# A fused spectral filter and spatial-shift MLP on one core: scales of three groups made at once, w2's scaling and memsets behind the second group's gelu scale, its statistics between the halves of w1

## The chip, the core and the metric

The kernel runs on one core of a Trainium2 chip. The metric is device time in microseconds of one execution. The kernel before takes 410.85 us (median of 3 runs, 410.72 to 411.11).

## What is computed

The input x has S = 2048 tokens of D = 448 features. The output is the sum of x, a spectral branch and an MLP branch:

```python
x = A_x
xn = _layernorm(x, axis=-1)
return x + _A_ref(xn, A_w_r, A_w_i) + _B_ref(xn, B_w1, B_w2, B_w3, B_w4)

def _A_ref(x, w_r, w_i):            # rfft2, times a complex weight, irfft2
    X = rfft2(x, axes=(-2, -1)) * (w_r + 1j * w_i)
    return irfft2(X, (S, D), axes=(-2, -1))

def _B_ref(x, w1, w2, w3, w4):
    h = _gelu(_layernorm(x, axis=-1) @ w1)
    # the four quarters of h's features are shifted by +1, -1, +2, -2 tokens
    hs = jnp.concatenate([g0, g1, g2, g3], axis=-1) @ w2
    x1 = x + hs
    h2 = _gelu(_layernorm(x1, axis=-1) @ w3) @ w4
    return x1 + h2
```

Only the first part of the MLP branch, up to the product with w2, is touched by the change. The spectral branch and the product with w3 and w4 follow it and overlap its end.

## The kernel before

**Tiling.** Token t sits in partition t // 16, so the 2048 tokens are 16 blocks of 128 partitions by 448 features. Blocks are worked on in four groups of four: `GRP = [[14, 15, 0, 1], [2, 3, 4, 5], [6, 7, 8, 9], [10, 11, 12, 13]]`. In this document they are called group 0 to group 3, as in the code. (The short description of the change counts them as words: its "third" group is group 2, its "second" is group 1.) All operands of matmuls are split into a high and a low float16 half, and a product is made of three passes: high by high, low by high, high by low. That is why most steps come in pairs, a copy on ScalarE (ACT) that makes the high half and a subtraction on VectorE (DVE) or GpSimd (POOL) that makes the low half.

**Steps of one group g, with their lines.**
- `stats` (L306, L307): mean and variance of each block on VectorE. The optional argument `pins` names, for each block, an instruction behind which its statistic is queued.
- `norm1` (L314 to L338): a first guess of the reciprocal root by integer arithmetic (`va`, `vy`: L323 to L326), the shift `nma` (L328), then the apply (L333 on ScalarE, L336 on VectorE or GpSimd, block by block as the list `apply` says). The result stands in place of x.
- `refine` (L345 to L354, all on GpSimd): ten small operations that make the root exact; the last one writes `gsc`, the scale that the gelu of this group's w1 product needs.
- `scales` (L358 to L365, all on GpSimd): eight small operations that make `cs`, by which the residual x is scaled when w2's product is added (L487), and the scale and bias with which the spectral branch later normalises x.
- `transpose_split` (called through `T1`; L387, L391, L401): sixteen transposes on TensorE, then high half on ScalarE and low half on VectorE. Group 3 goes through `turn` instead (L868 to L871), with a transpose by DMA.
- `w1_in` (L427): the product with w1, eleven matmuls for one block. A call for a part of the feature tiles does a part of it. The four units of group 0 keep their partial sums in the four banks of `first`.
- `w1_unit` (L467 to L478): gelu on ScalarE, high half on ScalarE (L468), low half on VectorE in two pieces (L470), both written, shifted, into `x2mem`; then one DMA transpose per finished block gives `h`.
- `w2_tile` (L486, L487): eleven matmuls with w2, then the residual on VectorE.
- `ln2`: the second layer norm of finished blocks and its DMA transposes (L506 to L522).

**Weights.** `squares` (L253, ScalarE) and `powers` (L258 to L267) turn the sum of squares of a weight into a power of two by which it is scaled: VectorE reduces (L258, marked "r1" or "r2" in the table `after`), TensorE adds over partitions by a product with ones (L260, "p1", "p2"), VectorE makes the exponent (L262 to L267, "e1", "e2"). The sum for w2 uses a free corner of the bank `first[0]`. `split_w` then makes the halves; for w2 and half of w1 GpSimd scales (L276, "ps"), ScalarE copies (L277) and GpSimd subtracts (L278). Two DMAs (L933, L934) copy parts of w2's high halves to other partitions.

**Shift over the ends.** `wrap_on` (L449 to L452) moves parts of group 0's result with two DMAs and clears one row of `pairs[0]` (L451) and all of `pairs[2]` (L452) on GpSimd; the areas are read and written again only when group 3's blocks are done (`wrap_back`).

**Order.** Each engine executes its own queue in order. The order in the queues comes from a planner that takes ready work in the order of the program and its priorities. `behind(key)` restricts it: every instruction that the block issues on the engine of a marked instruction is queued after that instruction. It is no wait of its own on another engine. `after["a1"]` stands for the last ScalarE copy and the last VectorE subtraction of group 1's transposes, `after["n", g]` for the last apply of group g on VectorE, `after["na", g]` for that on ScalarE, and `after["b0"]` for the last operations of `ln2([0, 1])`. SP's queue issues all DMAs.

Of the kernel before, what the change touches and what calls it, by code (L numbers as in the profile page):

```python
# [36 lines left out]
PIN = [("a3",), ("a3",), ("a3",), ("a3",)]  # L37
# [88 lines left out]
def body(tc, nc, x, wf, w1, w2, w3, w4, c_g, c_n, c_small, out):  # L126
# [185 lines left out]
    xn_scale, xn_bias = {}, {}  # L312

    def norm1(g, apply, pins=None):  # L314

        bs = GRP[g]
        n, b0 = len(bs), bs[0]
        mv = pc.tile([128, 4, 2], F32, name=f"mva{b0}")
        stats([xb(b) for b in bs], f"a{b0}", mv, pins)
        a = pc.tile([128, 2 * n], F32, name=f"va{b0}")  # L320
        yi = pc.tile([128, 2 * n], I32, name=f"vy{b0}")
        y = yi.bitcast(F32)
        V.tensor_scalar(out=a[:, n:], in0=mv[:, :n, 1], scalar1=1.0 + EPS, scalar2=EPS * EPS, op0=ALU.mult, op1=ALU.add)  # L323
        V.tensor_scalar(out=a[:, 0:n], in0=mv[:, :n, 1], scalar1=EPS, scalar2=None, op0=ALU.add)
        V.tensor_single_scalar(yi, a.bitcast(I32), 1, op=ALU.logical_shift_right)
        V.tensor_scalar(out=yi, in0=yi, scalar1=-1, scalar2=0x5F3759DF, op0=ALU.mult, op1=ALU.add)  # L326
        nm = pc.tile([128, n], F32, name=f"nma{b0}")
        i = V.scalar_tensor_tensor(out=nm, in0=mv[:, :n, 0], scalar=-1.0, in1=y[:, n:], op0=ALU.mult, op1=ALU.mult)  # L328
        after["c", g] = (i.ins,)
        for k, b in enumerate(bs):  # L330
            y_, m_ = y[:, n + k:n + k + 1], nm[:, k:k + 1]
            if apply[k] is A:
                i = A.activation(out=xb(b), in_=xb(b), func=AF.Identity, scale=y_, bias=m_)  # L333
                after["na", g] = (i.ins,)
            else:
                i = apply[k].tensor_scalar(out=xb(b), in0=xb(b), scalar1=y_, scalar2=m_, op0=ALU.mult, op1=ALU.add)  # L336
                if apply[k] is V:
                    after["n", g] = (i.ins,)  # L338

        q, z = (pc.tile([128, 2 * n], F32, tag=f"v{t}", bufs=2, name=f"v{t}{b0}") for t in "qz")  # L340
        w, r = (pc.tile([128, 2 * n], F32, name=f"v{t}{b0}") for t in "wr")
        nm1 = pc.tile([128, n], F32, name=f"nm{b0}")

        def refine():
            P.tensor_tensor(out=q, in0=y, in1=y, op=ALU.mult)  # L345
            P.tensor_tensor(out=q, in0=q, in1=a, op=ALU.mult)
            P.tensor_scalar(out=w, in0=q, scalar1=-10.0 / 3.0, scalar2=None, op0=ALU.add)
            P.tensor_tensor(out=w, in0=w, in1=q, op=ALU.mult)
            P.tensor_scalar(out=w, in0=w, scalar1=5.0, scalar2=None, op0=ALU.add)
            P.tensor_tensor(out=z, in0=w, in1=w, op=ALU.mult)  # L350
            P.tensor_tensor(out=z, in0=z, in1=q, op=ALU.mult)
            P.tensor_scalar(out=z, in0=z, scalar1=-0.5 * 0.375 ** 3, scalar2=1.5 * 0.375, op0=ALU.mult, op1=ALU.add)
            P.tensor_tensor(out=r, in0=z, in1=w, op=ALU.mult)
            P.tensor_scalar(out=gsc[:, 4 * g:4 * g + 4], in0=r[:, n:], scalar1=r1, scalar2=None, op0=ALU.mult)  # L354

        def scales():
            c, r1st, u = cs[:, 4 * g:4 * g + 4], w[:, 0:n], w[:, n:]
            P.tensor_tensor(out=r1st, in0=r[:, 0:n], in1=y[:, 0:n], op=ALU.mult)  # L358
            P.tensor_tensor(out=u, in0=r[:, n:], in1=r[:, n:], op=ALU.mult)
            P.tensor_tensor(out=c, in0=y[:, n:], in1=a[:, n:], op=ALU.mult)  # L360
            P.tensor_tensor(out=c, in0=c, in1=u, op=ALU.mult)
            P.tensor_tensor(out=c, in0=c, in1=r1st, op=ALU.mult)
            P.tensor_scalar(out=c, in0=c, scalar1=s12[:, 0:1], scalar2=None, op0=ALU.mult)
            P.tensor_tensor(out=nm1, in0=mv[:, :n, 0], in1=r1st, op=ALU.mult)
            P.tensor_scalar(out=nm1, in0=nm1, scalar1=-1.0, scalar2=None, op0=ALU.mult)  # L365
            for k, b in enumerate(bs):
                xn_scale[b], xn_bias[b] = r1st[:, k:k + 1], nm1[:, k:k + 1]
        return refine, scales
# [11 lines left out]
    def transpose_split(srcs, dst, key, ts=range(4), at=0, tags=("tr",) * 4, late=None):  # L380
        c = slice(128 * at, 128 * at + 128 * len(srcs))
        for t in ts:
            pt = bank(tags[t], f"pt{key}{t}")
            w = 128 if t < 3 else 64
            with behind("T", key) if ("T", key) in after else contextlib.nullcontext():
                for i, s in enumerate(srcs):
                    m = T.transpose(pt[:w, 128 * i:128 * i + 128], s[:, 128 * t:128 * t + w], ident)  # L387
# [3 lines left out]
            i = A.activation(out=dst[:w, t, c], in_=pt, func=AF.Copy)  # L391
            todo.append((key, t, i, lo, pt, dst[:w, t, c]))
        if late is None:
            low()

    todo = []

    def low():
        while todo:
            key, t, i, lo, pt, hi = todo.pop(0)  # L400
            j = V.tensor_tensor(out=lo, in0=pt, in1=hi, op=ALU.subtract)  # L401
            after[key, t] = after[key] = i.ins, j.ins
# [18 lines left out]
    def w1_in(g, units, ts, passes=range(3)):  # L421
        for p in passes:
            for t in ts:
                for i, pm in units:
                    wi, xi = ((0, 0), (0, 4), (4, 0))[p]
                    if t < 3 or p != 1:
                        T.matmul(pm[:, :D], xTs[g][:, xi + t, 128 * i:128 * i + 128], w1p[:, wi + t],  # L427
                                 start=t == 0 and p == 0, stop=t == 3 and p == 2)
# [20 lines left out]
    def wrap_on():  # L449
        move(pairs[1], pairs[0], -1)  # L450
        P.memset(pairs[0][0:1], 0.0)  # L451
        P.memset(pairs[2], 0.0)  # L452
# [403 lines left out]
    def T1(g, ts=range(4), late=None):  # L856
        if g not in xTs:
            xTs[g] = p1.tile([128, 7, 512], F16, tag="xT", bufs=2, name=f"xT{g}")
        transpose_split([xb(b) for b in GRP[g]], xTs[g], f"a{g}", ts,
                        tags=("mm", "mm", "tr", "tr") if g == 2 else ("tr", "tr", "acc", "acc"), late=late)  # L860
# [23 lines left out]
    n1 = [norm1(0, [P, V, A, V])]  # L884
    T1(0, range(1), True)
# [3 lines left out]
    with behind("e1"):  # L889
        low()  # L890
    for t in range(4):
        if t >= 1:
            with behind("p1"):
                T1(0, [t])
# [6 lines left out]
    n = 1  # L901
    for unit in list(enumerate(first))[:n]:
        w1_in(0, [unit], [2, 3])
    with behind("ps"):
        n1[0][0]()
    n1.append(norm1(1, [P, V, A, V], [("n", 0), ("r1",), ("a0", 0), ("a0", 1)]))
# [13 lines left out]
    n1[1][0]()  # L920
# [20 lines left out]
    n1[2][0]()  # L941
    for n in n1:
        n[1]()
# [16 lines left out]
    n1[0][0]()  # L960
    n1[0][1]()
# [153 lines left out]
```

## Time and profile before

| | |
|---|---|
| median of 3 runs | 410.85 us |
| the profiled execution | 410.88 us |
| its span on the core | 409.1 us |
| granted TensorE clock | 0.999 |
| busy: TensorE, VectorE, ScalarE, GpSimd | 400.4, 336.9, 256.1, 103.2 us |
| the first real matmul of w1 | at 12.44 us |
| DMA moved | 52.07 MB |

In the profile's rows PE is TensorE's matmul and PEld its weight load, DVE is VectorE, ACT ScalarE, POOL GpSimd, SP the queue that issues DMAs. A row of the time-ordered view has the start and the length in us, engine, line, operation, what it writes and reads, the shape, and how many like it were merged; in brackets stands how long the engine was idle before it and what ended the idle time. A row that merges several instructions covers the time from the first start to the last end. A row of the table by stages gives the stretch, its length, then busy time and number of instructions for PE, PEld, DVE, ACT and POOL, the granted clock, the share of DMA time, and GB/s. Names of buffers: `mva` mean and variance, `va` and `vy` the guess of the root, `nma` the shift, `vq`, `vz`, `vw`, `vr` the refinement, `pta` a bank of transposes, `xT` the transposed x, `w1s` and `w2s` weights as loaded, `w1p` and `w2p` their halves, `xr` a scratch target of the squares.

### The profile page before, as it was taken

Reading aid. Unit: us, or ns where it says so; the run is one execution under the profiler, and the core shown is the slowest. Engines: PE = TensorE matmul, PEld = TensorE weight load, DVE = VectorE, ACT = ScalarE, POOL = GpSimd, SP = SyncE. Lnnn points to the kernel's source line nnn. Section 1 sums busy time; section 2 is a strip of 40 time slices with the busy share of each in tenths; the row PEclk is TensorE's granted clock in tenths of the full one; section 3 lists DMA queues with packets and bytes.
Section 4 is the critical chain, followed back from the end, with each engine's and each line's share of the span. In section 5 each row is a group of like instructions: output and inputs, shape, how many; then the busy total and the mean of one; then the engine's idle time right before and its main releaser. Section 6 shows DMA issues by size and latency. Waiting matters only on the chain.

```text
span 409.1 us, 8749 instructions
## 1 busy us (share of the span) xinstructions
PE 400.4 (98%) x3391; PEld 297.5 (73%) x3391; DVE 336.9 (82%) x702; ACT 256.1 (63%) x434; POOL 103.2 (25%) x173
## 2 busy tenths in 40 slices
PE   8899999999999999999999999999999999999996
PEld 3455545765667777877787887877777779998995
DVE  5998999999856895998798888956899999965645
ACT  4689699882558866655598878863454445453431
POOL 7787630112145948310022111110000000000000
PEclk9999999999999999999999999999999999999999
DMA  8977995558779652536255666510011023100101
GB/s 275 373 286 139 238 177 140 110 115 178 102 200 292 219 151 77 182 136 179 68 144 143 155 149 164 146 31 13 22 70 69 24 85 96 46 2 2 45 2 45
DMA packets 54596, 52.07 MB, mean 127 GB/s; under 512 B 35678, under 2 KB 48542, under 8 KB 54556
## 3 DMA queue, kind: packets, MB, share of 16 engines
q1 hardware_dynamic: 54556, 51.53, 46.4%
q8 instruction: 26, 0.43, 0.4%
q14 instruction: 14, 0.11, 0.1%
HBM read 38.28 MB, written 3.67 MB: 103 GB/s over the span
## 4 chain that ended last, share of the span: by engine, by line
PE 86%; DVE 5%; DMA 3%; POOL 2%; ACT 1%; SPq 1%; issue 1%
PE pw L407 33%; PE acc L816 23%; PE pw L486 6%; PE side L786 4%; PE acc L786 3%; PE pu L675 3%; PE ps L575 3%; PE pe L696 2%; PE pp L630 2%; PE px L647 2%; PE py L717 2%; PE pw L427 2%; DMA xt<-x 1%; DVE sta L306 1%; DVE xT L401 1%; DMA w2p<-w2p 1%
## 5 line engine op out<-in xcount | busy, mean ns | idle before, releaser
L407 PE MATMUL pw<-x2mem,w3p 128*128 128x256 f16 x1232 | 152.0, 273 | 0.0
L407 PEld LDWEIGHTS <-w3p 128*128 128x128 f16 x1232 | 119.0, 98 | 19.6
L816 PE MATMUL acc<-w4p,hf 128*128 128x448 f16 (+1 forms) x516 | 104.2, 348 | 0.0
L816 PEld LDWEIGHTS <-hf 128*128 128x128 f16 x516 | 50.1, 98 | 37.5
L734 ACT ACTIVATE pw<-pw,pe 128x512 f32<-128x512 f32 x42 | 27.5, 654 | 31.7 <-PE pw L407 31.6
L737 DVE SCALAR_TENSOR_TENSOR hf<-pw,h,hf 128x512 f16<-128x512 f32 x42 | 31.3, 745 | 12.7 <-ACT hf L736 12.4
L486 PE MATMUL pw<-w2p,h 128*128 128x448 f16 x176 | 35.7, 353 | 1.6 <-DMA h<-x2mem 1.2
L427 PE MATMUL pw<-w1p,xT 128*128 128x448 f16 x176 | 34.8, 352 | 0.7 <-ACT w1p L280 0.4
L656 POOL TENSOR_TENSOR z<-te 128x450 f32<-128x450 f32 x16 | 15.7, 981 | 70.7 <-DVE te L654 65.8
L736 ACT ACTIVATE hf<-pw,h 128x512 f16<-128x512 f32 x42 | 28.8, 685 | 5.0 <-PE acc L816 4.0
L486 PEld LDWEIGHTS <-h 128*128 128x128 f16 x176 | 17.1, 98 | 17.2 <-DMA h<-x2mem 1.9
L427 PEld LDWEIGHTS <-xT 128*128 128x128 f16 x176 | 17.2, 98 | 16.6 <-issue 1.1
L752 ACT ACTIVATE hz<-g,h 128x896 f16<-128x896 f32 x14 | 14.6, 1042 | 22.9 <-DVE g L749 22.9
L786 PEld LDWEIGHTS <-hz 128*128 128x128 f16 x294 | 28.2, 98 | 0.6
L637 ACT ACTIVATE pf<-pp 64x450 f16<-64x450 f32 x32 | 17.3, 542 | 12.6 <-DVE pf L638 9.6
L638 DVE TENSOR_TENSOR pf<-pp,pf 64x450 f16<-64x450 f32 x32 | 19.9, 622 | 5.1 <-ACT pf L637 4.8
L753 DVE SCALAR_TENSOR_TENSOR hz<-g,h,hz 128x896 f16<-128x896 f32 x14 | 16.1, 1147 | 6.7 <-ACT hz L752 6.7
L558 POOL TENSOR_TENSOR f<-xr 128x452 f32<-128x452 f32 x16 | 19.7, 1250 | 0.6
L566 DVE TENSOR_TENSOR xh<-f,xh 128x452 f16<-128x452 f32 x16 | 14.3, 916 | 4.9 <-ACT xh L565 4.9
L652 ACT ACTIVATE te<-px 64x450 f32<-64x450 f32 x32 | 17.3, 540 | 1.2 <-PE px L647 0.6
L746 ACT ACTIVATE g<-pw,pe 128x512 f32<-128x512 f32 x14 | 9.6, 683 | 11.4 <-PE pw L407 11.4
L555 POOL TENSOR_TENSOR xr<-xf 128x452 f32<-128x452 f32 x8 | 9.2, 1154 | 24.4 <-issue 17.6
(188 smaller groups left out, 712.5 us busy)
## 6 DMA issues: line engine op xcount, KB each, us to landing
wc<-wf SPq DMA_DIRECT2D x32, 225.0 KB, 3.7
wl<-wf SPq DMA_DIRECT2D x8, 450.0 KB, 4.2
xt<-x SPq DMA_DIRECT2D x8, 448.0 KB, 7.8
xf<-x SPq DMA_DIRECT2D x8, 448.0 KB, 4.9
loads<-x SPq DMA_DIRECT2D x7, 448.0 KB, 3.5
out<-xt SPq DMA_DIRECT2D x13, 224.0 KB, 1.9
w3raw<-w SPq DMA_DIRECT2D x3, 896.0 KB, 11.3
gn<-c_g SPq DMA_DIRECT2D x16, 128.0 KB, 3.1
```

The lines of the kernel that those rows point to most:

```text
L407: T.matmul(ps_out, wp[:, wi + t, cols], xT[:, xi + t, tok], start=t == 0 and wi + xi == 0, stop=t == 3 and wi == 4)
L427: T.matmul(pm[:, :D], xTs[g][:, xi + t, 128 * i:128 * i + 128], w1p[:, wi + t], start=t == 0 and p == 0, stop=t == 3 and p == 2)
L486: T.matmul(pm[:, :D], h[:, k], w2p[:, w], start=n == 0, stop=n == 10)
L558: P.tensor_tensor(out=f[:, :, k:k + 2].rearrange("p b s d -> p s b d"), in0=u[:, :, 0], in1=u[:, :, 1], op=op)
L637: A.activation(out=hi, in_=src, func=AF.Copy)
L638: V.tensor_tensor(out=lo, in0=src, in1=hi, op=ALU.subtract)
L652: A.activation(out=e[64 * h:64 * h + 64], in_=px_[64 - 64 * h:128 - 64 * h, :2 * DF], func=AF.Copy)
L734: A.activation(out=pm, in_=pm, func=AF.Gelu_apprx_tanh, scale=r3)
L736: i = A.activation(out=h[:, 0], in_=pm, func=AF.Copy, scale=h3)
L737: j = V.scalar_tensor_tensor(out=h[:, 1], in0=pm, scalar=h3, in1=h[:, 0], op0=ALU.mult, op1=ALU.subtract)
L786: m = T.matmul(to, h[:, hi, 128 * blk:128 * blk + 128], b[wi], start=new and n == 0, stop=n == 2 and (last if blk in (2, 5, 3, 0) else end ...
L816: m = T.matmul(to, h[:, hi, o:o + 128], w4p[0][:, wi, f, r], start=first and f % 2 == 0 and n == 0, stop=end and f % 2 == 1 and n == 2, sk ...
```

## The change

- `mva`, `va`, `vy`, `vw`, `vr` and the two shifts become one tile each for all groups; a group uses a slice.
- `scales(g, n)` works on n groups at once: one call for groups 0 to 2 after group 2's `refine`, instead of three calls there, and one for group 3.
- Group 0 is applied by `[P,V,P,V]` instead of `[P,V,A,V]`, and all its transposes stand behind "p1"; the first four had stood ahead of it, with their low half behind "e1".
- Group 1's statistics are pinned behind "r1", the first copy of group 0's transposes, and the first two halves of w1, instead of group 0's last apply, "r1" and the first two copies. Group 2's are pinned behind "e2" as well.
- Two units of group 0 (n = 2, before 1) finish their w1 product ahead of "p2"; the last two, before three, stand behind "p2" and not behind group 1's transposes. "p2" itself stands behind the matmuls of the second unit.
- w2's scaling on GpSimd is queued behind group 1's `gsc`, and the two memsets of `wrap_on` behind w2's last low half.
- w3's splits and the squares of w4 beside them stand behind "b0" and not behind "a3".

```diff
-PIN = [("a3",), ("a3",), ("a3",), ("a3",)]
+PIN = [("b0",), ("b0",), ("b0",), ("b0",)]
...
+    mva = pc.tile([128, NB, 2], F32, name="mva")
+    va, vw, vr = (pc.tile([128, 2, NB], F32, name=f"v{t}") for t in "awr")
+    vyi = pc.tile([128, 2, NB], I32, name="vy")
...
-            P.tensor_scalar(out=gsc[:, 4 * g:4 * g + 4], in0=r[:, n:], scalar1=r1, scalar2=None, op0=ALU.mult)
-
-        def scales():
-            c, r1st, u = cs[:, 4 * g:4 * g + 4], w[:, 0:n], w[:, n:]
...
+            i = P.tensor_scalar(out=gsc[:, c], in0=r[:, 1], scalar1=r1, scalar2=None, op0=ALU.mult)
+            after["g", g] = (i.ins,)
+        return refine
+
+    def scales(g, n):
+
+        o = slice(4 * g, 4 * g + 4 * n)
+        c, r1st, u, y, r = cs[:, o], vw[:, 0, o], vw[:, 1, o], vy[:, :, o], vr[:, :, o]
+        P.tensor_tensor(out=r1st, in0=r[:, 0], in1=y[:, 0], op=ALU.mult)
+        P.tensor_tensor(out=u, in0=r[:, 1], in1=r[:, 1], op=ALU.mult)
+        P.tensor_tensor(out=c, in0=y[:, 1], in1=va[:, 1, o], op=ALU.mult)
+        P.tensor_tensor(out=c, in0=c, in1=u, op=ALU.mult)
+        P.tensor_tensor(out=c, in0=c, in1=r1st, op=ALU.mult)
+        P.tensor_scalar(out=c, in0=c, scalar1=s12[:, 0:1], scalar2=None, op0=ALU.mult)
+        P.tensor_tensor(out=nm1[:, o], in0=mva[:, o, 0], in1=r1st, op=ALU.mult)
+        P.tensor_scalar(out=nm1[:, o], in0=nm1[:, o], scalar1=-1.0, scalar2=None, op0=ALU.mult)
...
     def wrap_on():
         move(pairs[1], pairs[0], -1)
-        P.memset(pairs[0][0:1], 0.0)
-        P.memset(pairs[2], 0.0)
...
-    n1 = [norm1(0, [P, V, A, V])]
-    T1(0, range(1), True)
+    n1 = [norm1(0, [P,V,P,V])]
     with behind("n", 0):
         s1, r1 = powers(m1, 4, "1", "mm")
     first = [bank("mm" if k < 2 else "sp", f"pw1_0{k}") for k in range(4)]
-    with behind("e1"):
-        low()
     for t in range(4):
-        if t >= 1:
-            with behind("p1"):
-                T1(0, [t])
+        with behind("p1"):
+            T1(0, [t])
...
-    n = 1
+    n = 2
...
-    n1.append(norm1(1, [P, V, A, V], [("n", 0), ("r1",), ("a0", 0), ("a0", 1)]))
+    n1.append(norm1(1, [P, V, A, V], [("r1",), ("a0", 0), ("w1", 0), ("w1", 1)]))
...
     with behind("T", "a1"):
-        for unit in list(enumerate(first))[n:]:
+        for unit in list(enumerate(first))[n:2]:
             w1_in(0, [unit], [2, 3])
-    with behind("n", 1):
+    with behind("n", 1), behind("u"):
         s2, r2 = powers(m2, 1, "2", first[0][:, 448:512])
+    with behind("p2"):
+        for unit in list(enumerate(first))[2:]:
+            w1_in(0, [unit], [2, 3])
...
     with behind("a1"):
-        n1.append(norm1(2, [P, V, A, P]))
+        n1.append(norm1(2, [P, V, A, P], [("e2",), ("e2",), ("e2",), ("e2",)]))
...
     wrap_on()
-    with behind("na", 2):
+    with behind("g", 1), behind("na", 2):
         for k in range(4):
             r = slice(0, 128 if k < 3 else 64)
-            split_w(w2p[r, k], w2p[r, 7 + k], w2s[r, k], s2[r], P)
+            after["w2", k] = split_w(w2p[r, k], w2p[r, 7 + k], w2s[r, k], s2[r], P)
         SY.dma_start(w2p[64:128, 3:7], w2p[0:64, 0:4])
         SY.dma_start(w2p[0:64, 4:7], w2p[64:128, 0:3])
+    with behind("w2", 3):
+        P.memset(pairs[0][0:1], 0.0)
+        P.memset(pairs[2], 0.0)
...
-    n1[2][0]()
-    for n in n1:
-        n[1]()
+    n1[2]()
+    scales(0, 3)
```

More of the change, by code (lines that the diff above doesn't have):

```diff
@@ L391, in transpose_split @@
             i = A.activation(out=dst[:w, t, c], in_=pt, func=AF.Copy)
[L392 to L401 removed]
+            j = V.tensor_tensor(out=lo, in0=pt, in1=dst[:w, t, c], op=ALU.subtract)
             after[key, t] = after[key] = i.ins, j.ins
@@ L426, in w1_in @@
                     if t < 3 or p != 1:
-                        T.matmul(pm[:, :D], xTs[g][:, xi + t, 128 * i:128 * i + 128], w1p[:, wi + t],
-                                 start=t == 0 and p == 0, stop=t == 3 and p == 2)
+                        m = T.matmul(pm[:, :D], xTs[g][:, xi + t, 128 * i:128 * i + 128], w1p[:, wi + t],
+                                     start=t == 0 and p == 0, stop=t == 3 and p == 2)
+        after["u"] = (m.ins,)
     def slot(b):
```

62 lines of the change are left out of this document (24 added, 38 removed).

## The prediction

> **What bounds the kernel now.** I read the page's busy times first, then the table by stages, then TensorE's waits, and last the time-ordered rows of each engine over the first 62 us, where every edited line runs.
>
> ```profile
> span 409.1 us, 8749 instructions
> PE 400.4 (98%) x3391; PEld 297.5 (73%) x3391; DVE 336.9 (82%) x702; ACT 256.1 (63%) x434; POOL 103.2 (25%) x173
> ```
> ```profile
> 9.16:24.80 15.64, 13.22 (x81) 8.29 (x81) 13.80 (x42) 11.61 (x23) 12.17 (x33) 1.00 1.03 379
> ...
> 37.69:58.35 20.66, 19.86 (x105) 10.03 (x104) 19.63 (x60) 17.19 (x28) 10.81 (x32) 1.00 1.00 208
> 58.35:120.00 61.65, 61.65 (x394) 38.50 (x395) 55.05 (x146) 44.90 (x71) 8.73 (x19) 1.00 0.68 143
> ```
>
> TensorE (second column) is full from 58.35 on: later time is a fixed amount of matmul. Only the idle before 58.35 can be won, unless the change starves TensorE later. That idle is short, and TensorE's rows in time order name each piece in brackets (how long, and what ended it):
>
> ```profile
> 10.32 0.38 PE L260 MATMUL pm<-pt,ones 128*128 128x1 f32 x2 [0.50 <-DVE pt L258]
> ...
> 12.44 1.67 PE L427 MATMUL pw<-w1p,xT 128*128 128x448 f16 x8 [0.37 <-ACT w1p L280]
> 14.46 4.13 PE L427 MATMUL pw<-w1p,xT 128*128 128x448 f16 x21 [0.34 <-DVE w1p L281]
> 19.34 0.38 PE L260 MATMUL pw<-pt,ones 128*128 128x1 f32 x2 [0.75 <-DVE pt L258]
> 20.18 1.97 PE L387 MATMUL pta<-ident,xt 128*128 128x128 f32 x16 [0.46 <-POOL xt L336]
> ...
> 35.12 1.31 PE L486 MATMUL pw<-w2p,h 128*128 128x448 f16 x6 [0.51 <-DMA h<-x2mem]
> ...
> 37.69 0.73 PE L486 MATMUL pw<-w2p,h 128*128 128x448 f16 x3 [0.45 <-DMA w2p<-w2p]
> ...
> 58.35 2.25 PE L486 MATMUL pw<-w2p,h 128*128 128x448 f16 x11 [0.68 <-DMA h<-x2mem]
> ```
>
> Together 4.06 us, the most that tidying can give. The 21 matmuls in 4.13 us give 0.197 us for one w1 matmul and 0.113 us (sixteen in 1.8 us, the last one's modelled end left out) for one transpose. Groups are numbered 0 to 3 in this text.
>
> **The change part by part.**
>
> *Group 0's fourth apply moves from ScalarE to GpSimd; the sum that scales w1 comes sooner.*
>
> ```profile
> 8.46 0.74 ACT L333 ACTIVATE xt<-xt,nma,vy 128x448 f32<-128x448 f32 x1
> 9.11 0.56 ACT L253 ACTIVATE xr<-w1s 64x448 f16<-64x448 f32 x1
> ```
> ```profile
> 8.09 1.26 DVE L336 TENSOR_SCALAR xt<-xt,vy,nma 128x448 f32<-128x448 f32 x2
> 8.16 0.94 POOL L336 TENSOR_SCALAR xt<-xt,vy,nma 128x448 f32<-128x448 f32 x1
> ...
> 10.12 0.14 DVE L258 TENSOR_REDUCE pt<-m 128x1 f32<-128x4 f32 x1
> ...
> 12.01 0.62 DVE L306 BATCH_NORM_STATS2 sta<-xt 128x6 f32<-128x448 f32 x1
> ...
> 13.19 0.62 DVE L306 BATCH_NORM_STATS2 sta<-xt 128x6 f32<-128x448 f32 x1
> 13.72 0.68 DVE L281 SCALAR_TENSOR_TENSOR w1p<-w1s,pe,w1p 128x448 f16<-128x448 f32 x1
> ...
> 20.87 0.60 ACT L391 ACTIVATE xT<-pta 128x512 f16<-128x512 f32 x1 [0.26 <-PE pta L387]
> ```
>
> Without L333 the fourth square starts 0.65 us earlier. The first statistic of group 1 is now pinned behind the reduction L258 and not ahead of it, so L258 starts when VectorE's applies end, 9.35 instead of 10.12: 0.77 us. Against it: GpSimd does two applies in a row, the second at the 0.71 us of group 1's (row below), and ends at 9.8, and all sixteen transposes now stand behind the small matmul. Four transposes later, near 10.4, ScalarE's first copy (L391, 0.60 us) can start; the copy of w1 is as long. The first w1 matmul comes at 11.6 if w1's copy goes second on ScalarE, at 12.2 if third, instead of 12.44: 0.2 to 0.8 us, I take **-0.5**. The 0.34 us wait for the low half L281 goes too (**-0.34**; bounds 0 and -0.34): two statistics stood ahead of it, and the new pins hold one of them back behind w1's halves.
>
> *n = 2: two units' tail matmuls ahead of the w2 sum, two behind it, none behind group 1's transposes.* Five more matmuls, 5 x 0.197 = 0.98 us, stand where TensorE waited 0.75 us, and ten (1.97 us) where it waited 0.46 us for GpSimd's apply of group 1. Both waits are covered: **-1.21**. But TensorE reaches the w2 sum at 18.59 - 0.84 + 0.98 = 18.7, and if VectorE's reduction stays where it is, it still waits until 19.34, 0.6 us. Two things pull it forward:
>
> ```profile
> 16.76 1.03 POOL L278 TENSOR_TENSOR w1p<-w1s,w1p 128x448 f16<-128x448 f32 x1
> ...
> 16.79 1.03 DVE L325 TENSOR_SCALAR vy<-va 128x8 int32<-128x8 int32 x1
> ...
> 18.32 0.20 POOL L358 TENSOR_TENSOR vw<-vr,vy 128x4 f32<-128x4 f32 x1
> ...
> 19.42 0.71 POOL L336 TENSOR_SCALAR xt<-xt,vy,nma 128x448 f32<-128x448 f32 x1
> ...
> 29.15 0.17 DVE L325 TENSOR_SCALAR vy<-va 128x8 int32<-128x8 int32 x1
> ```
>
> L325 takes 0.17 us at 29.15; at 16.79 it was held until GpSimd's L278 ended. And L336 stood behind scale operations of group 0 (from L358 at 18.32 on, up to 1.1 us) that now run after group 2. I take half: **+0.3** left of the wait (0 to 0.6).
>
> The price: before, fifteen tail matmuls covered the evacuation of group 1's transposes. Now ten do if the transposes go first, none if they go last. Uncovered, TensorE waits for four copies of 0.6 us and their low halves less the transposes' own time, about 1 us. Bounds 0 and +1.0; program order puts the transposes first, so **+0.3**.
>
> *Three groups' scales at once; w2's scaling behind group 1's gelu scale; memsets behind w2's split.*
>
> ```profile
> 5.55 1.60 POOL L452 MEMSET x2mem<- 128x1792 f16 x1
> ...
> 22.68 1.25 POOL L276 TENSOR_SCALAR w2s<-w2s,pe 128x448 f32<-128x448 f32 x2
> ...
> 25.46 0.20 POOL L353 TENSOR_TENSOR vr<-vz,vw 128x8 f32<-128x8 f32 x1
> ...
> 27.49 1.58 POOL L451 MEMSET x2mem<- 1x1792 f16 x1
> ...
> 28.09 1.01 DVE L323 TENSOR_SCALAR va<-mva 128x4 f32<-128x4 f32 x1
> ...
> 30.42 1.96 ACT L277 ACTIVATE w2p<-w2s 128x448 f16<-128x448 f32 x4
> ...
> 32.90 3.01 POOL L278 TENSOR_TENSOR w2p<-w2s,w2p 128x448 f16<-128x448 f32 x3
> ...
> 37.63 0.29 POOL L354 TENSOR_SCALAR gsc<-vr,pe 128x4 f32<-128x4 f32 x1
> ...
> 39.13 0.29 POOL L363 TENSOR_SCALAR cs<-cs,s 128x4 f32<-128x4 f32 x1
> ...
> 40.97 0.66 DVE L487 SCALAR_TENSOR_TENSOR xt<-xt,cs,pw 128x448 f32<-128x448 f32 x1
> ```
>
> Sixteen small GpSimd operations vanish (24 become 8; at 0.20 to 0.29 us, L358 and L363, 3 to 4.6 us). A 12-wide one is not in the trace; 8-wide L353 and 4-wide L358 both take 0.20, so I price it the same, and at 0.30 as the upper end. w2's scaling (four of 0.63 us) can wait: its reader L277 starts at 30.42, 6.5 us after it ended. With the memset gone from 27.5, L323 and L324 shed the 0.9 us by which they were held, so group 2's chain (statistics, apply, w2's high halves, w2p's DMA, the first transpose of h) moves at least as far as TensorE does. Hence I leave the waits of 0.51 and 0.45 as they are: **0** (bounds -0.96 and, if w2's halves stay, +1.0). The DMAs of w2p and the shift, and SP's order of them, are not pinned anew.
>
> The memsets add 1.58 + 1.60 us between w2's last low half (32.90 + 3.01 = 35.9) and the rest of group 2's refinement (to the end of L354, 2.0 us) and the scales (to the end of L363, 1.5 us). If the low halves end 1.45 us earlier, cs is ready at 34.45 + 3.2 + 2.0 + 1.6 = 41.25; L487 asks for it at 40.97 - 1.45 = 39.5. So L487 waits, and in VectorE's queue group 3's aggregates and normalisation, and with them SP's run of DMA transposes, may stand behind it:
>
> ```profile
> 43.38 0.15 DVE L323 TENSOR_SCALAR va<-mva 128x4 f32<-128x4 f32 x1
> ...
> 49.79 2.56 SPq L871 DMA_TRANSPOSE xT<-x  x2
> ...
> 55.17 1.25 SPq L478 DMA_TRANSPOSE h<-x2mem  x1
> ```
>
> That run is full from 49.79 to the h that TensorE waits for at 58.35. Loss 0 if group 3's work goes ahead of L487, up to 1.45 + 0.3 = 1.75 us if behind. I take **0**: group 3's statistics come first in the program.
>
> The GPSIMD Engine Reference of the Trainium skill (Specifications) says that GpSimd contends with VectorE only for instructions in a two-port mode or with two SBUF inputs. The held L323 and L325 agree. By it the memsets' new place is free beside PSUM evacuations, and costs up to 1.6 us only if it meets group 3's short scalar chain at 43.4.
>
> *The rest.* e2 in front of group 2's statistics changes nothing, since these already stand behind group 1's last low half. Moving w3's splits behind b0 instead of a3 changes no more: they need s3, made from all of w3's squares, the last of which is pinned behind a unit of group 2. What can move is the squares of w4 in the same blocks: one that gets ahead of group 3's copies on ScalarE costs that chain some 1.1 us (twice the columns of L253 above); one that fills a gap costs nothing. I take **0**, since the copies come first in the program.
>
> **Sum:** -0.5 - 0.34 - 1.21 + 0.3 + 0.3 = -1.45 us. The profiled execution took 410.88, 1.78 over its span; 410.88 - 1.45 = 409.43, and it lies 0.03 over the median. I say **409.4**.
>
> **The rivals.**
>
> *Given back at SP (410.8).* TensorE comes early and waits for the same h at 58.35: 0.68 becomes about 2.1 us. For it: VectorE is busy 19.63 of 20.66 us there, and the cs arithmetic above. Against: with cs late, group 3's chain has a free VectorE.
>
> *Slower: GpSimd's pile-up (412.2).* If the early chain does not move, cs comes at 35.9 + 3.2 + 2.0 + 1.6 = 42.7, 1.7 us after L487's start; with L487 ahead of group 3's aggregates all of SP's run slips by as much, less some 0.3 us won elsewhere: +1.4. It decides from where cs passes 41.0 while group 3 stands behind L487. For: the memsets come earlier in the program than refinement and scales. Against: the 0.9 us hold on L323 is gone in any case.
>
> *More (408.0).* The w2 sum moves a full microsecond (-0.3 more), the evacuation is covered (-0.3), and the three DMA waits shrink by half of 1.64 us: -2.9.
>
> *Pins without effect.* If the order on VectorE comes out as before, only the n = 2 part and ScalarE's freed time act: about -0.7, 410.2; it belongs to the same class as no change.
>
> **How the numbers follow.** Forecast 0.42, more 0.13, no change (both kinds) 0.20, slower 0.25. A difference under 0.2% (0.8 us) cannot be told from none. So faster 0.55, same 0.20, slower 0.25. The forecast's own range is 408.7 to 410.0; with the cases of both signs, 407.7 to 412.1.
>
> **What would show it.** Right: first w1 matmul near 12, the w2 sum near 18.9, no wait there above 0.4, group 1's unit matmuls done 1 to 2 us before 33.15, and the 58.35 row earlier by the same. Wrong: a wait of w1 matmuls for L401 or L391 near 22, cs (L363) after 42 with L487 just behind it, a hold on L323 near 43, or the row at 58.35 unmoved behind a longer wait for h.

## The result, and the profile after

| | before | changed |
|---|---|---|
| median, side by side | 410.98 us (410.72 to 411.59, 4 runs) | 408.26 us (408.05 to 408.32, 4 runs) |
| profiled execution | 410.88 | 408.05 |
| its span | 409.1 | 406.3 |

The changed kernel takes 0.9931 of the time before, with an interval of 0.9914 to 0.9948: faster by 2.7 us, where 1.45 was forecast.

TensorE's rows in time order, of the profile after (row form as before; L389 are the transposes, L420 the product with w1, L478 that with w2):

```profile
9.54 0.38 PE L260 MATMUL pm<-pt,ones 128*128 128x1 f32 x2 [0.37 <-DVE pt L258]
...
11.72 6.92 PE L420 MATMUL pw<-w1p,xT 128*128 128x448 f16 x34
19.30 1.97 PE L389 MATMUL pta<-ident,xt 128*128 128x128 f32 x16 [0.66 <-POOL xt L336]
21.10 0.28 PE L260 MATMUL pw<-pt,ones 128*128 128x1 f32 x2
21.24 10.37 PE L420 MATMUL pw<-w1p,xT 128*128 128x448 f16 x54
31.45 1.91 PE L389 MATMUL pta<-ident,xt 128*128 128x128 f32 x16
33.72 1.31 PE L478 MATMUL pw<-w2p,h 128*128 128x448 f16 x6 [0.36 <-DMA h<-x2mem]
...
37.39 2.26 PE L478 MATMUL pw<-w2p,h 128*128 128x448 f16 x11 [0.28 <-DMA h<-x2mem]
...
46.67 4.33 PE L478 MATMUL pw<-w2p,h 128*128 128x448 f16 x22
51.21 2.25 PE L478 MATMUL pw<-w2p,h 128*128 128x448 f16 x11 [0.22 <-DMA h<-x2mem]
...
53.44 2.24 PE L420 MATMUL pw<-w1p,xT 128*128 128x448 f16 x11
55.52 2.25 PE L478 MATMUL pw<-w2p,h 128*128 128x448 f16 x11
```

Two more rows of before, to lay beside these (33.15, the transposes of group 2, answers to 31.45, 55.43 to 53.44, 58.35 of the prediction to 55.52):

```profile
33.15 1.47 PE L387 MATMUL pta<-ident,xt 128*128 128x128 f32 x12
...
55.43 2.24 PE L427 MATMUL pw<-w1p,xT 128*128 128x448 f16 x11
```

So the lead over before is 0.72 us at the first w1 matmul, 1.70 at 31.45, 1.99 at 53.44 and 2.83 at 55.52. The span is shorter by 2.8: all of it was won before 58 us, and the lead keeps its size from there on. The brackets of these two executions say where:

- 0.72 at the first matmul, and 0.34 because no wait for L281 stands among the 34 matmuls.
- Behind them, waits of 0.75 and 0.46 became one of 0.66: 0.55. With 0.09 in gaps too short for a bracket this makes the 1.70.
- Waits for h and w2's parts, 0.51 + 0.45, became 0.36 + 0.28 + 0.22: 0.10, and 0.19 more in short gaps.
- The 0.68 for h at 58.35 is gone, with 0.16 around it: 0.84.

GpSimd's rows of the changed kernel, and some of VectorE's, hold the part of the change that the prediction feared (the first row of each belongs to group 1 and is used further below):

```profile
18.30 0.94 POOL L336 TENSOR_SCALAR xt<-xt,vy,nma 128x448 f32<-128x448 f32 x1
...
35.15 1.58 POOL L927 MEMSET x2mem<- 1x1792 f16 x1
36.68 1.58 POOL L928 MEMSET x2mem<- 128x1792 f16 x1
...
40.30 0.21 POOL L360 TENSOR_TENSOR vw<-vr,vy 128x12 f32<-128x12 f32 x1
...
41.81 3.19 POOL L336 TENSOR_SCALAR xt<-xt,vy,nma 128x448 f32<-128x448 f32 x4
...
45.16 0.31 POOL L365 TENSOR_SCALAR cs<-cs,s 128x12 f32<-128x12 f32 x1
```
```profile
16.92 0.58 DVE L324 TENSOR_SCALAR va<-mva 128x4 f32<-128x4 f32 x1
...
39.99 0.17 DVE L324 TENSOR_SCALAR va<-mva 128x4 f32<-128x4 f32 x1
...
45.51 1.27 DVE L479 SCALAR_TENSOR_TENSOR xt<-xt,cs,pw 128x448 f32<-128x448 f32 x2 [0.29 <-POOL cs L365]
```

The scales `cs` are ready at 45.47, 6 us later than before (39.42), and the residuals L479 start right behind them. But group 3's chain went ahead of the residuals: its L324 runs at 39.99, against 43.38 before (L323 there). TensorE feels nothing: the third tile of w2 needs the PSUM bank that the first residual frees, near 46.2 (estimated as half of the row), and its turn comes only at 46.67. SP's queue of the changed kernel shows what group 3's early chain does to the order there:

```profile
44.65 1.82 SPq L863 DMA_TRANSPOSE xT<-x  x1
46.57 1.83 SPq L470 DMA_TRANSPOSE h<-x2mem  x1
48.51 2.85 SPq L863 DMA_TRANSPOSE xT<-x  x2
51.45 1.25 SPq L470 DMA_TRANSPOSE h<-x2mem  x1
...
59.80 2.56 SPq L514 DMA_TRANSPOSE x2mem<-y  x2
```

Before, the h that TensorE waited for at 58.35 was issued at 55.17 behind two transposes of x and two of the second norm:

```profile
52.52 2.56 SPq L522 DMA_TRANSPOSE x2mem<-y  x2
```

Now it is issued at 51.45, with no transpose of the second norm ahead of it.

### The profile page after: what moved, and what is told of

It is laid out like the page before. It is cut to its first block, busy times and chain, and to the rows that moved or that the text cites. A ratio compares the mean times of both kernels' runs of the same rounds, so it can differ in the third digit from the quotient of the medians.

```text
span 406.3 us, 8732 instructions
## 1 busy us (share of the span) xinstructions
PE 399.9 (98%) x3391; PEld 297.2 (73%) x3391; DVE 333.6 (82%) x702; ACT 255.1 (63%) x433; POOL 100.4 (25%) x158
## 2 busy tenths in 40 slices
DMA packets 54596, 52.07 MB, mean 128 GB/s; under 512 B 35678, under 2 KB 48542, under 8 KB 54556
## 4 chain that ended last, share of the span: by engine, by line
PE 87%; POOL 5%; DMA 2%; DVE 2%; ACT 2%; issue 1%; SPq 0%; POOLq 0%; ACTq 0%
PE pw L400 33%; PE acc L808 23%; PE pw L478 6%; PE side L778 4%; PE acc L778 3%; PE pu L667 3%; PE ps L567 3%; PE pe L688 2%; PE pp L622 2%; PE px L639 2%; PE py L709 2%; PE pw L420 2%; DMA w1s<-w 1%; POOL xt L336 1%; DMA h<-x2mem 1%
## 5 line engine op out<-in xcount | busy, mean ns | idle before, releaser
L400 PEld LDWEIGHTS <-w3p 128*128 128x128 f16 x1232 | 118.9, 98 | 19.3
L729 DVE SCALAR_TENSOR_TENSOR hf<-pw,h,hf 128x512 f16<-128x512 f32 x42 | 31.3, 746 | 12.9 <-ACT hf L728 12.7
L478 PE MATMUL pw<-w2p,h 128*128 128x448 f16 x176 | 35.8, 353 | 0.9 <-DMA h<-x2mem 0.9
L420 PE MATMUL pw<-w1p,xT 128*128 128x448 f16 x176 | 34.9, 352 | 0.1
L478 PEld LDWEIGHTS <-h 128*128 128x128 f16 x176 | 17.0, 98 | 17.0 <-DMA h<-x2mem 2.0
L420 PEld LDWEIGHTS <-xT 128*128 128x128 f16 x176 | 17.1, 99 | 16.1 <-DVE xT L394 0.4
```

What stands on the lines that cost most here:

```text
L400: T.matmul(ps_out, wp[:, wi + t, cols], xT[:, xi + t, tok], start=t == 0 and wi + xi == 0, stop=t == 3 and wi == 4)
L420: m = T.matmul(pm[:, :D], xTs[g][:, xi + t, 128 * i:128 * i + 128], w1p[:, wi + t], start=t == 0 and p == 0, stop=t == 3 and p == 2)
L478: T.matmul(pm[:, :D], h[:, k], w2p[:, w], start=n == 0, stop=n == 10)
L729: j = V.scalar_tensor_tensor(out=h[:, 1], in0=pm, scalar=h3, in1=h[:, 0], op0=ALU.mult, op1=ALU.subtract)
```

## The experiments

Each is the changed kernel with the edit shown, except the last of the first part; each ratio is to the kernel before on the same chip, which took 410.9 to 411.0 us there.

### GpSimd's small operations

**Scales group by group, as early as the data allow.** The merging undone.

```diff
-    scales(0, 3)
+    for g in range(3):
+        scales(g, 1)
```

> The changed kernel (span 406.3 us, 2.8 less than before) with the scales of groups 0, 1 and 2 as three separate calls again at the same place of the program, so that the planner may put each where it is ready. Theory A (the late cs let group 3's normalisation go ahead of the first residual on VectorE, which filled SP's run earlier and took away the 0.68 us wait for h at 58 us): cs of group 0 is there before 30 us again, the first residual (L479) stands ahead of group 3's scalar chain, L324 of group 3 goes from 39.99 to 42 or later, and the wait for h near 55 to 58 us comes back; time 0.7 to 1.2 us over the changed kernel's 408.26 us, 409.0 to 409.5. Theory B (GpSimd's relief: six small operations of group 0 in front of group 1's apply): group 1's transposes start about 1.2 us later than 19.30 and the time is 1.0 to 1.3 us over, with group 3's chain in its early place. Theory C (only the earlier arrival of w1's sum and the two-unit order count): within 0.4 us of 408.26.

Measured 409.78 us (409.36 to 411.86), ratio 0.9982 [0.9969, 0.9994]: 1.5 us of the gain gone. GpSimd's and TensorE's rows of this run:

```profile
18.51 0.21 POOL L360 TENSOR_TENSOR vw<-vr,vy 128x4 f32<-128x4 f32 x1
...
20.44 0.71 POOL L336 TENSOR_SCALAR xt<-xt,vy,nma 128x448 f32<-128x448 f32 x1
```
```profile
21.21 1.97 PE L389 MATMUL pta<-ident,xt 128*128 128x128 f32 x16 [2.10 <-POOL xt L336]
```

Small operations of group 0 stand ahead of group 1's apply again, from 18.51 on. The apply starts at 20.44 instead of 18.30, and the wait of 0.66 becomes 2.10: 1.44 us more, about the size of the loss. The first residual went ahead of group 3's chain, as theory A had it (L479 at 41.50, L324 at 44.00), but no wait for h near 55 to 58 us came back, and the time lies above the ranges of both theories.

**The same 24 operations, but all behind group 2's refinement.** The place kept, only the merging undone.

```diff
-    scales(0, 3)
+    with behind("g", 2):
+        for g in range(3):
+            scales(g, 1)
```

> The changed kernel with three separate calls of scales as in scales_apart, but queued on GpSimd behind group 2's gelu scale, where the one call stands. The number of GpSimd operations is that of before, their place that of the change. Theory A: cs is as late as in the changed kernel or later, group 3's chain goes first, 408.0 to 408.7 us. Theory B asks only for the place ahead of group 1's apply to be free, which it is: the same. If it is the merging itself that counts (sixteen operations of 0.2 us in front of group 3's four applies), the applies start up to 4 us later than 41.81 and the time is 1 us or more over 408.26.

Measured 412.52 us (411.3 to 413.49), ratio 1.0037 [1.0023, 1.0051]: slower than before. The first scale `cs` comes at 48.44 here, and the third tile of w2 has run into it:

```profile
48.47 1.27 DVE L479 SCALAR_TENSOR_TENSOR xt<-xt,cs,pw 128x448 f32<-128x448 f32 x2 [0.36 <-POOL cs L365]
```
```profile
49.20 6.00 PE L478 MATMUL pw<-w2p,h 128*128 128x448 f16 x22 [2.38 <-DVE xt L479]
```

A wait of 2.38 us, and then 22 matmuls take 6.00 us that take 4.33 in the changed kernel (row at 46.67). So the late place alone loses; the changed kernel bears it because merging takes sixteen operations, and 3 us, out of the stretch ahead of `cs`.

**Two groups' scales early, behind group 1's gelu scale.**

```diff
+    with behind("g", 1):
+        scales(0, 2)
     for k in range(4):
         w1_unit(1, k)
...
-    scales(0, 3)
+    scales(2, 1)
```

> The changed kernel with the scales of groups 0 and 1 made together behind group 1's gelu scale, those of group 2 alone in the old place. cs of the first residuals is there 15 us earlier than in the changed kernel, but no scale operation stands ahead of group 1's apply. memsets_back (cs at 39.2, residual ahead of group 3's chain, 408.56) has spoken against theory A; if the 1.5 us of scales_apart came only from the six operations ahead of group 1's apply (theory B), this one stays within 0.4 us of 408.26 with transposes of group 1 at 19.3; if an early cs costs, it is at 409 or above.

Measured 408.84 us (408.51 to 408.95), ratio 0.9945 [0.9933, 0.9958]. Nothing of the scales stands ahead of group 1's apply, TensorE's wait there is 0.73 us, and all but 0.6 us of the gain stays (theory B allowed 0.4; the interval overlaps that of the changed kernel). Late scales are not needed for most of it; scales out of the way at 18 to 20 us are.

**The kernel before with this one part.** Its scales, group by group, queued behind group 1's apply; nothing else of the change.

```diff
-                if apply[k] is V:
-                    after["n", g] = (i.ins,)
+                after["n" if apply[k] is V else "np", g] = (i.ins,)
...
     for n in n1:
-        n[1]()
+        with behind("np", 1):
+            n[1]()
```

> The kernel before with one part alone: the scales of groups 0 to 2, still one group at a time, are queued on GpSimd behind group 1's apply. Theory B (the small operations ahead of that apply cost the time there): the apply runs near 18.6 instead of 19.42, the waits of 0.75 and 0.46 us at 18.6 to 20.2 fall below 0.4 together; if nothing else moves 410.0 to 410.4. Rival: the planner now queues the w2 sum behind group 1's transposes on TensorE, so s2 and w2's scaling come later and TensorE waits for w2's parts between 33 and 40: 410.8 to 412.5.

Measured 411.05 us (410.77 to 411.35), ratio 1.0004 [0.9995, 1.0013]: nothing won. The apply did move up, from 19.42 to 18.63, and the planner then put the w2 sum behind the transposes on TensorE:

```profile
19.81 1.97 PE L386 MATMUL pta<-ident,xt 128*128 128x128 f32 x16 [1.11 <-POOL xt L336]
21.61 3.00 PE L426 MATMUL pw<-w1p,xT 128*128 128x448 f16 x15
24.45 0.28 PE L260 MATMUL pw<-pt,ones 128*128 128x1 f32 x2
```

The two waits there fell from 1.21 to 1.11 us only, since five matmuls fewer than in the changed kernel (29, not 34) stand ahead of the transposes and the apply lasts 1.13 us here. And the sum is 5 us later, w2's parts with it; the three waits for h and w2's parts grew from 1.64 to 2.28 us. Alone the part wins nothing; it pays only beside the other edits.

### The memsets, the late scales and the pins

**The memsets back in `wrap_on`.**

```diff
         move(pairs[1], pairs[0], -1)
+        P.memset(pairs[0][0:1], 0.0)
+        P.memset(pairs[2], 0.0)
...
-    with behind("w2", 3):
-        P.memset(pairs[0][0:1], 0.0)
-        P.memset(pairs[2], 0.0)
```

> The changed kernel with the two memsets of the wrap in their old place in the program (behind nothing). GpSimd then has 3.2 us less between w2's last low half and the scales, so cs would be there up to 3 us before 45.5. Theory A: if cs is early enough for the planner to put the first residual ahead of group 3's chain, part of the gain goes, 408.6 to 409.3 us; if not, within 0.3 us of 408.26. My GpSimd pile-up theory of the prediction (memsets in that place cost time) says faster than the changed kernel by 0.3 to 1 us.

Measured 408.56 us (408.36 to 408.6), ratio 0.9942 [0.993, 0.9954], an interval that overlaps the changed kernel's. `cs` is ready at 39.18, the residuals go ahead of group 3 as before, and SP's run of transposes begins at 48.07:

```profile
48.07 2.56 SPq L865 DMA_TRANSPOSE xT<-x  x2
50.80 1.22 SPq L516 DMA_TRANSPOSE x2mem<-y  x1
52.07 1.29 SPq L472 DMA_TRANSPOSE h<-x2mem  x1
```

There is still no wait for h near 55: its issue at 52.07 stands behind one transpose of the second norm, not two. So neither the late scales nor group 3's early chain is needed to take the 0.68 us away. Which edit turned this order stays open: in no run of the changed kernel with a part taken back did both transposes stand ahead of this h again. In the run before this one, the kernel before with its scales moved, neither did, but all four transposes of x, and a wait of 0.76 us for h stayed.

**w3's splits and w4's squares behind a3 again.**

```diff
-PIN = [("b0",), ("b0",), ("b0",), ("b0",)]
+PIN = [("a3",), ("a3",), ("a3",), ("a3",)]
```

> The changed kernel with w3's splits and the squares beside them behind a3 again. My prediction priced this edit at nothing: within 0.25 us of 408.26. If the place of those squares on ScalarE is what removed the wait for h near 58 us, 0.4 to 0.9 us over, with that wait back.

Measured 415.83 us (415.36 to 417.0), ratio 1.0121 [1.0107, 1.0135]: 7.6 us slower than the changed kernel, far outside both ranges, by one constant. ScalarE's rows, first of this run and then of the changed kernel:

```profile
58.77 7.57 ACT L280 ACTIVATE w3p<-w3raw,pe 128x896 f16<-128x896 f32 x8
66.23 0.62 ACT L460 ACTIVATE x2mem<-pw,h 128x448 f16<-128x448 f32 x1
66.75 2.35 ACT L509 ACTIVATE y<-y,vs 128x448 f16<-128x448 f32 x4
```
```profile
56.81 0.62 ACT L460 ACTIVATE x2mem<-pw,h 128x448 f16<-128x448 f32 x1
57.67 1.23 ACT L509 ACTIVATE y<-y,vs 128x448 f16<-128x448 f32 x2 [0.23 <-DVE vs L298]
58.80 1.96 ACT L280 ACTIVATE w3p<-w3raw,pe 128x896 f16<-128x896 f32 x2
```

With the pin at a3 all eight splits of w3 go ahead of a unit's L460 and of the second norm's L509; on VectorE the L281 stand ahead in the same way. TensorE pays at 73.69, and the w2 product behind the wait then takes 4.29 us instead of 2.25:

```profile
73.69 4.29 PE L478 MATMUL pw<-w2p,h 128*128 128x448 f16 x11 [4.99 <-DVE y L512]
```

The bracket names L512, which happened to end last. The product reads h, and its h was issued on SP at 70.65, behind the late L460 and its low half (70.14): 3.0 us ahead, as the 3.2 us from 55.17 to 58.35 before. So the late L460 is the likelier cause, though no run separates the two.

**Both together**, to see whether the pin is bad in itself.

> The memsets back in their old place (408.56 measured) and, beside it, w3's splits and w4's squares pinned behind a3 again (alone, that pin cost 415.83). Theory P: the two pins are the same place as long as the residuals and the second norm of the first blocks go ahead of group 3's copies, as they do with the old place of the memsets; only cs being late makes a3 an earlier place. Then 408.56 within 0.4, and no wait of TensorE for L512 between 60 and 80 us above 0.3. Rival: the pin at a3 is bad in itself in the changed kernel (early transposes of group 3): 412 to 416 with the wait of about 5 us near 74 again.

Measured 408.56 us (408.23 to 408.8), ratio 0.9945 [0.9932, 0.9958], the same as with the memsets back alone. With the memsets in their old place the second norm's copies (47.90 to 49.12) go ahead of the last two of group 3's (51.21 and 52.20), and under either pin w3's splits begin at the same place of ScalarE's queue (at 60.47 with b0, at 60.27 with a3). In the changed kernel, with its late `cs`, group 3's last copies (46.56 to 47.60) come some 10 us ahead of the second norm's (57.67), and so does a3. The new pin is the companion that the late scales need.

### The first matmuls

**Group 0 applied as before, and group 1's statistics pinned as before.**

```diff
-    n1 = [norm1(0, [P,V,P,V])]
+    n1 = [norm1(0, [P, V, A, V])]
...
-[("r1",), ("a0", 0), ("w1", 0), ("w1", 1)]
+[("n", 0), ("r1",), ("a0", 0), ("a0", 1)]
```

> The changed kernel with group 0 applied by P, V, A, V and group 1's statistics pinned as before (behind group 0's last apply, r1 and the first two copies). TensorE's queue is the same, instruction for instruction. The sum for w1 comes about 0.75 us later and the first w1 matmul at 12.4 to 12.9 instead of 11.72. Theory D (the first term of my sum is real, -0.5 to -0.84): 0.5 to 0.9 us over 408.26, 408.8 to 409.2. Theory E (that gain only lengthens the wait for group 1's apply on GpSimd, 0.66 us in the changed kernel, which then shrinks instead): group 1's transposes stay at 19.0 to 19.5 and the time is within 0.3 us of 408.26.

Measured 409.32 us (409.12 to 410.35), ratio 0.9963 [0.995, 0.9975]: 1.06 us of the gain gone. That rules out theory E (0.3) and is a little more than theory D (0.9). The transposes stay behind "p1" here, so it is not the whole edit of group 0's start. Its profile is that of the longest run (410.35), so only the order (and, in the last section, the clock) is read from it: a statistic of group 1 stands ahead of L258 on VectorE again, and in this execution it waited for its block of x (0.72 us), so that the small matmul came at 10.81.

### How many units ahead of the w2 sum

**One (n = 1), as before.**

```diff
-    n = 2
+    n = 1
...
-        for unit in list(enumerate(first))[n:2]:
+        for unit in list(enumerate(first))[n:]:
             w1_in(0, [unit], [2, 3])
-    with behind("n", 1), behind("u"):
+    with behind("n", 1):
...
-    with behind("p2"):
-        for unit in list(enumerate(first))[2:]:
-            w1_in(0, [unit], [2, 3])
```

> The changed kernel with the old order of group 0's tail matmuls: one unit ahead of the w2 sum, three behind group 1's transposes, the w2 sum not behind the second unit. In the changed kernel 34 matmuls end at 18.64 and the transposes wait 0.66 us until 19.30 for GpSimd's apply. With five matmuls fewer ahead the wait grows to about 1.6 us, so 0.95 us over 408.26 if TensorE's work is what counts (409.1 to 409.4); within 0.3 us if the stage is bound further down by the chain of groups 2 and 3.

Measured 409.05 us (408.85 to 409.41), ratio 0.9955 [0.9942, 0.9968]. The wait for GpSimd's apply grows from 0.66 to 1.49, and the time by 0.8: the second unit is worth what it covers. Not all is as before, though: the w2 sum comes at 24.38, behind the transposes and fifteen matmuls (21.10 in the changed kernel), and a low half (L394) costs 0.28 at 17.11.

**Three**, the last unit alone behind "p2".

```diff
-    n = 2
+    n = 3
...
-        for unit in list(enumerate(first))[2:]:
+        for unit in list(enumerate(first))[n:]:
```

> The changed kernel with three units' tail matmuls ahead of group 1's transposes and one behind the w2 sum. Five more matmuls (0.97 us) stand in front of the transposes, where TensorE waits 0.66 us for GpSimd's apply. Theory E' (that wait is idle time which any ready matmul fills): the wait goes, transposes start 0.3 us later, all the same work is done 0.66 us sooner, 407.6 to 408.0. Theory F (five matmuls are too few to cover the evacuation of group 1's transposes, the price I put at up to 1 us): a wait of w1 matmuls for L394 or L393 near 22.5 us takes the gain back, 408.1 to 408.8.

Measured 411.84 us (410.97 to 412.39), ratio 1.0017 [1.0008, 1.0026]. The wait at 19.3 is covered, and the kernel is 3.6 us slower than the changed one, worse than either theory:

```profile
19.52 1.97 PE L389 MATMUL pta<-ident,xt 128*128 128x128 f32 x16
...
35.67 2.07 PE L478 MATMUL pw<-w2p,h 128*128 128x448 f16 x10 [1.13 <-DMA h<-x2mem]
...
53.95 2.25 PE L478 MATMUL pw<-w2p,h 128*128 128x448 f16 x11 [1.83 <-DMA h<-x2mem]
```

A wait of 0.99 us at 133.64, for VectorE's L729, is new as well. On ScalarE a square of w3 (1.7 us) had got ahead of unit (1,3)'s L460, and I took that for the cause.

**Three, with w3's first two squares held behind that unit.**

```diff
-        with behind(*(("a2",), ("a2",), (2, 0), (2, 1))[k]):
+        with behind(*(("a2",), ("a2",), (2, 0), (2, 1))[k]), behind(1, 3):
```

> Three units of group 0 finished ahead of the w2 sum (411.84 measured), and the first two squares of w3 (L253, 1.7 us each on ScalarE) held behind unit (1,3)'s copy L460, which they had overtaken (36.65 instead of 34.73). Theory S, the overtaking made that h late and with it everything on SP behind it: the wait of 1.83 us near 54 falls below 0.5, the wait of 1.13 near 35.7 stays (w2's high halves are still later and its two DMAs behind a second h): 410.0 to 410.6. Theory V, VectorE's order (all four low halves of group 1 ahead of e2, and so group 2's statistics 0.4 to 1.2 us later): the waits stay, 411.4 to 412.2. Theory W, all of the loss was the squares: 407.5 to 408.3.

Measured 411.65 us (410.64 to 412.99), ratio 1.0017 [1.0005, 1.0029]. L460 moved from 36.65 to 34.85 and both waits stayed (1.11 and 1.77; the one at 133.75 is 1.31), so that was not it. Time and waits are those of theory V, VectorE's order, but it was not tested by itself. What is still different from the changed kernel is VectorE's order: group 2's aggregates stand between low halves of h (L462, from 26.67 on) and its L324 runs at 28.40 and not 27.28; and SP issues a second h ahead of w2's DMAs. Which of these costs how much stays open.

**Two and a half**, an attempt to cover just the 0.66: the third unit's first three tail matmuls ahead of "p2", with the squares held as above.

```diff
+    w1_in(0, [(2, first[2])], [2])
     with behind("n", 1), behind("u"):
...
-            w1_in(0, [unit], [2, 3])
+            w1_in(0, [unit], [2, 3] if unit[0] > 2 else [3])
...
-    for k in range(4):
-        w1_unit(1, k)
+    for k in range(2):
+        w1_unit(1, k)
+    with behind("na", 2):
+        for k in range(2, 4):
+            w1_unit(1, k)
```

> An attempt at a faster version: of the third unit's five tail matmuls three go ahead of the w2 sum (0.6 us, the size of the wait for GpSimd's apply at 19.3), two behind; the squares of w3 held behind unit (1,3), and units (1,2) and (1,3) held on ScalarE behind group 2's apply so that w2's high halves and DMAs keep their place. If the covered wait comes through: 407.5 to 408.0, transposes of group 1 without a wait above 0.2 and the waits for h together no more than the changed kernel's 0.9. If the shift in order eats it, as with three units: 408.5 to 410.5 with waits for h of 2 us or more between 33 and 58.

Measured 411.25 us (410.51 to 413.08), ratio 1.0012 [1.0002, 1.0022]. The wait at 19 fell to 0.21, and 1.51 for a low half (L394) at 34.65 and 1.39 and 0.65 for h replaced it; the time lies above both ranges. None of the variants beat the changed kernel.

The losses do not add: scales apart, group 0 as before and one unit together cost 3.4 us, and the change won 2.7. All three act on the same stretch before the transposes at 19.30.

## Why the prediction was right, and where its sizes were off

**The mechanism was right for the larger part.** The time was won by tidying TensorE's waits before 58 us. Of the 2.83 in the profiles, 1.70 was won ahead of 31.45, by the start of the w1 matmuls, L281's wait and the two waits at 19 to 20 us, where the sum had its 1.45. That these two are so near is in part luck, since the terms miss in both directions: 0.22, 0.30 and 0.09 (short gaps) too little, 0.36 too much. The other 1.13 came from waits for DMA that were priced at nothing. 408.26 lies in the whole range but below the forecast's own (408.7 to 410.0).

**The signs.** The first w1 matmul came near 12 (11.72), and the lead at the row of 33.15 was 1 to 2 us (1.70). But the w2 sum came at 21.10 and not near 18.9, a wait of 0.66 stood there, and the lead at the row of 58.35 was 2.83, not the same. One sign of being wrong came too: `cs` after 42 with the residual just behind it (45.47), and it did no harm.

**First w1 matmul, -0.5.** -0.72 in the profile. In the ten other runs with the same edits to group 0's start it came between 11.48 and 12.14 (median 11.99), in two with the old start at 12.44 and 12.55: 0.3 to 1.1 earlier. So -0.5 is nearer to the typical run (-0.45) than the profile's -0.72. Taking two of these edits back cost 1.06 over all. **L281, -0.34:** as forecast.

**n = 2, -1.21, and +0.3 left of a wait.** Together -0.55 and not -0.91. This step had the w2 sum first, and the next one the transposes, which can't both be. In fact the transposes went first and waited 0.66 for GpSimd, whose apply at 18.30 follows `nma` and lasts 0.94, not 0.71. And `nma` was late itself, since group 1's L324 took 0.58 at 16.92, until GpSimd's L278 ended, where group 3's took 0.17. The unit that I priced by its cover was worth 0.8 (one unit).

**Evacuation, +0.3.** Not there: the transposes did go ahead of the ten matmuls, and 54 matmuls run from 21.24 without a bracket. I took a part of the upper bound, although I had named the order that decides; that gave away 0.3.

**Waits for DMA, priced 0.** Here lies the largest error of the sum. The two of 0.51 and 0.45 kept to it within 0.1 (0.29 with short gaps). The one of 0.68 at 58.35 vanished: 0.84 with its gap. I had named it as the end of SP's full run and asked only whether that run gets later; the change also altered the order in it, and with the second norm's transposes no longer both ahead of it the h left SP earlier. The rival "More" had half of this wait gone, and its 408.0 is nearer to the result than my 409.4, and it had the evacuation covered; its w2 sum a microsecond earlier did not come. Why the order on SP turned, the runs leave open.

**Pile-up, +0 taken, 412.2 as a rival.** The place was right and the point of decision wrong. `cs` came at 45.47, beyond my 41.25 and the rival's 42.7, because GpSimd's four applies of group 3 (41.81 to 45.0) also went ahead of its last step; and group 3's chain did not stand behind L479. What decides is the bank for w2's third tile, near 46.7. Scales apart in the late place pass it by 2.4 us and take 412.52, close to the rival's price by another way.

**PIN, priced 0.** It changes nothing with the memsets in their old place, as I argued, but 7.6 us with late scales. I had priced it against the kernel before, where a3 comes after b0, and not against the order that the change itself makes.

**The price of the small operations.** 128x12 took 0.20 to 0.25 us, as priced, and 0.31 the one with a scalar from a tile (L365); the hold on group 2's L324 is gone (0.17 us at 27.28). Where the prediction cited the Trainium skill (GPSIMD Engine Reference, Specifications) on when GpSimd contends with VectorE, this trace agrees as to the memsets. They ran from 35.15 to 38.26; under them VectorE's evacuations at 35.92 and 36.76 took 0.80 (two L462) and 0.68 us (L394), as at 20.24 and 20.97 (0.81 and 0.68), and group 3's L324 came behind them. That the held L323 and L325 agree as well was argued, not shown: each has one input in SBUF, and no row says whether it ran in a two-port mode.

## What to carry to other kernels

When a step is moved later, ask for the first thing that can't wait for it (here a PSUM bank, half a microsecond away) rather than for what stands next in the queue, and price the change's pins against the new order, not the old. Of a full DMA queue, look at the order as well as the start: one transfer less ahead of the awaited one can be as good as an earlier run. And a wait covered by moving work can come back as a different order further on, which cost more here (3.6 us) than the wait (0.66).

## What the runs showed of the hardware

A wait of TensorE of more than 2 us cost more than itself in three cases of four. The table by stages, with the granted clock in the column before the DMA share, for some four microseconds behind four waits: 2.10 us (scales apart), 2.26 us (group 0 as before, ahead of 10.81), 2.38 us (scales apart and late), 4.99 us (pin at a3):

```profile
21.20:25.20 4.00, 3.99 (x29) 3.02 (x30) 2.87 (x7) 3.30 (x7) 2.92 (x15) 1.00 1.03 411
```
```profile
10.81:14.40 3.59, 3.59 (x19) 3.36 (x20) 2.94 (x11) 2.33 (x5) 2.14 (x5) 0.55 1.06 319
```
```profile
49.20:53.20 4.00, 4.00 (x13) 1.66 (x13) 3.45 (x10) 4.00 (x8) 3.25 (x14) 0.60 1.01 227
```
```profile
73.69:77.70 4.01, 4.01 (x11) 1.64 (x12) 2.92 (x9) 0.67 (x1) 0.83 (x2) 0.50 0.85 145
```

The first keeps the full clock, the others fall to 0.55, 0.60 and 0.50. The fall does not come with the wait's end. In slices of one microsecond from 49.20 on, scales apart and late show 0.91, 0.50, 0.50, 0.50 and 0.89: if the clock is either 1.00 or 0.50, it fell some 0.8 us after the wait's end and was back 3.4 us later (estimated from these slices). With the pin at a3, 72.00 to 73.69 shows 0.74, a fall ahead of the wait's end. So something besides a wait's length decides, and four waits give no limit.

The lower clock adds 1.7 us to the wait of 2.38 (6.00 instead of 4.33), and 2.0 to that of 4.99 (4.29 instead of 2.25). The Trainium skill (TensorE: Matmul & The Clock Gate, Why this matters for your kernels) advises to keep idle gaps below about 3 us; here 2.26 us was enough, and 2.10 was not.
